# A convolution and a gated feed-forward layer on one core: reordering the kernel's first 20 microseconds

## The chip, the cores and the metric

One core of a Trainium2 chip runs the kernel. The metric is device time in microseconds (us), the median of several executions. Times inside the kernel are counted from the first instruction of one profiled execution. The engines are named PE or TensorE (matrix multiply; PEld are its weight loads), DVE or VectorE, ACT or ScalarE, POOL or GpSimd, and SP or SyncE, which here issues DMAs.

## The reference

```python
# x: (8, 4096, 192) float32, weight: (8, 7); moe_w_in: (192, 2048), moe_w_out: (2048, 192), moe_beta: (2048,)
w = softmax(weight, axis=-1)                          # 7 taps for each of 8 heads (24 channels a head)
x_pad = concatenate([zeros((8, 6, 192)), x], axis=1)  # causal: six rows of zeros ahead
conv[b, s, h, g] = sum_k w[h, k] * x_pad[b, s + k, h, g]
h = conv.reshape(32768, 192) @ moe_w_in
g = h * sigmoid(moe_beta * h)
out = g @ moe_w_out
```

## The kernel before, in words

The 32768 rows are cut into two streams (`s` = 0 and 1) of 16384 rows, worked side by side: stream 0 lives on partitions 0 to 63, stream 1 on 64 to 127. The 192 channels are split into three groups of 64 (`kk`), and the 2048 hidden columns into 16 chunks of 128 (`fc`).

Rows go in *steps*. Steps 0 and 1 have 128 rows of each stream, step 2 has 256, some more have 256 and 384, and the rest 512. For each step `i` and each unit `u` the first product (`mm1_pair` in steps 0 to 2, L326; `mm1` after them, L344) writes a PSUM buffer `ph`, of which there are two, and ScalarE applies Silu with the scale beta from `ph` to `g` (L330, L349). The second product (`mm2`, L377; later `mm2_quarters`, L423) sums over the 16 chunks in banks `po`; since the activation computes Silu(beta h) and not h sigmoid(beta h), `w_out` is divided by beta beforehand (`scale_w_out`, L274, one instruction for a chunk).

From step 3 on VectorE computes the convolution (`conv_ops`, L302 and L304) while TensorE multiplies. For the first 512 rows this would be too late, so TensorE does it: blocks 0 to 3 of 128 rows are transposed by TensorE (`transpose_0`, L216), copied to `xr` (`take_0`, L222 on ScalarE or L224 on VectorE), multiplied by seven diagonal matrices, one for each tap (`conv_0`, L230: a pair of matmuls for a tap, one for each stream), and brought to `xcp` with the softmax's denominator (`evac_0`, L239, L241). Block 0 feeds step 0, block 1 step 1, blocks 2 and 3 step 2. The diagonals (L200) come from the taps: a matmul spreads `taps` over the partitions (L191), VectorE takes the maximum (L193), ScalarE the exponential (L196).

Every instruction is pinned to its program order on its engine (`pin`). `first_tile(i, u)` is an order written out by hand: it says which pieces of convolution, evacuation and scaling stand behind unit `u` of steps 0 and 1. `first_mm2` does the same for the second product of steps 0 and 1: the table's entries name a pair of output blocks, the units (step, u) behind which its matmuls stand, and the cuts of the 16 chunks between them.

At the start `warm(n, cols)` issues `n` matmuls of a constant (L184) whose result nobody reads: fillers. Two stand ahead of the tap matmul (nine of 256 columns and one of 128), three between it and the transposes of block 0, and eight behind those.

The loads at the start: SP issues the taps, block 0 of stream 0, beta, and block 1; ACT issues block 0 of stream 1. GpSimd issues, in this order, `w_in` for its own half of the partitions (columns 0:256 and 256:640 of each half), blocks 2 and 3 of x, `w_in` 640:1024, four pieces of `w_out` (L157), the rows of the next tile (L159, L81), and then four copies of `w_in` from one half of the partitions to the other (L116). Steps 0 to 2 take each column from the half into which it was loaded; from step 3 on both halves are read.

Of the kernel before, what the change touches and what calls it, by code (L numbers as in the profile page):

```python
# [19 lines left out]
def kernel(  # L20
# [9 lines left out]
    nc = tc.nc  # L30

    B, S, D = x.shape
    H, K = weight.shape
# [3 lines left out]
    NF = F // 128  # L37
    NK = 3
    Q = D // NK
    NS = 2  # L40
# [3 lines left out]
    NB = TILE // 128  # L44

    def pin(ins):

        return tc.keep_in_program_order(ins)
# [35 lines left out]
    def cast_x(j, s, b0=0, b1=NB, eng=None):  # L84
        if j not in xbf_of:
            xbf_of[j] = xbf_pool.tile([128, NB, NK, NS, Q], BF16, name="xb")
        pin((eng or nc.vector).tensor_copy(  # L87
            xbf_of[j][:, b0:b1, :, s, :].rearrange("p b k q -> p k b q"),
            xf_of[j][:, b0:b1, s, :].rearrange("p b (q k) -> p k b q", k=NK)))

    def new_xt(j):
        xt_of[j] = xt_pool.tile([128, NK, LEAD + TILE], BF16, name="xt")

    def transpose_x(j, b):
        if j not in xt_of:
            new_xt(j)
        c = LEAD + 128 * b
        pin(nc.sync.dma_start_transpose(
            out=xt_of[j][:, :, c:c + 128],
            in_=xbf_of[j][:, b, :, :, :].rearrange("p k s q -> p (k s q)")))  # L100
# [4 lines left out]
    w_out_f = consts.tile([128, NF, D], FP32, name="w_out_f")  # L105
    w_out_s = consts.tile([128, NF, D], BF16, name="w_out_s")
    w_out_v = moe_w_out.rearrange("(c p) d -> p c d", p=128)

    def half_of(s):
        return slice(64 * s, 64 * s + 64)  # L110

    def load_w_in(s, f0, f1):
        pin(nc.gpsimd.dma_start(out=w_in_s[half_of(s), :, f0:f1], in_=w_in_v[:, :, f0:f1]))

    def copy_w_in(s, f0, f1):
        pin(nc.gpsimd.dma_start(out=w_in_s[half_of(1 - s), :, f0:f1], in_=w_in_s[half_of(s), :, f0:f1]))  # L116
# [3 lines left out]
    xb0 = consts.tile([128, 2, NS, D], BF16, name="xb0")  # L120
    xb1 = consts.tile([128, 2, NS, D], BF16, name="xb1")
    taps = consts.tile([H, K], FP32, name="taps")
    pin(nc.sync.dma_start(out=taps, in_=weight))
    for s, eng in enumerate((nc.sync, nc.scalar)):
        pin(eng.dma_start(out=x0[:, 0, s, :], in_=xs[s, 0:128, :]))
    beta16 = consts.tile([NF, 128], FP32, name="beta16")
    pin(nc.sync.dma_start(out=beta16, in_=moe_beta.rearrange("(c p) -> c p", p=128)))
    HF = F // 2

    def load_x0(b, eng):  # L130
        pin(eng.dma_start(out=x0[:, b, :, :] if b < 2 else xb0[:, b - 2, :, :],
                          in_=xs[:, 128 * b:128 * b + 128, :].rearrange("s p d -> p s d")))
# [14 lines left out]
                                pattern=[[0, NS], [-1, H], [0, Q // H]], channel_multiplier=1))  # L147
    pin(nc.gpsimd.affine_select(out=ident, in_=ident, compare_op=ALU.not_equal, fill=1.0,
                                base=0, pattern=[[-1, 128]], channel_multiplier=1))
    for f0, f1 in ((0, 256), (256, 640), (640, HF)):  # L150
        for s in range(NS):
            load_w_in(s, HF * s + f0, HF * s + f1)
        if f0 == 256:
            for b in range(2, NB):
                load_x0(b, nc.gpsimd)
    for c in range(0, NF, 4):
        pin(nc.gpsimd.dma_start(out=w_out_f[:, c:c + 4, :], in_=w_out_v[:, c:c + 4, :]))  # L157
    for s in range(NS):
        pin(nc.gpsimd.dma_start(out=xb1[:, :, s, :],  # L159
                                in_=xs[s, TILE:TILE + 256, :].rearrange("(b p) d -> p b d", p=128)))  # L160
# [12 lines left out]
    def po_banks():  # L173
        return [po_bank(), po_bank()]
# [7 lines left out]
    def warm(n, cols):  # L182
        for _ in range(n):
            pin(nc.tensor.matmul(idle[:, 0, 0:cols], ones[:, 0:128], ones[:, 0:cols], start=True, stop=True))  # L184

    warm(9, 256)
    warm(1, 128)
    cv0 = psum_h.tile([128, 2, TILE], FP32, name="ph")
    nmax = consts.tile([128, 1], FP32, name="nmax")
    tap_ps = cv0[:, 1, 0:K]  # L190
    pin(nc.tensor.matmul(tap_ps, sel.rearrange("h s g j -> h (s g j)"), taps, start=True, stop=True))  # L191
    warm(3, 128)
    pin(nc.vector.tensor_reduce(out=nmax, in_=tap_ps, axis=AX.X, op=ALU.max, negate=True))  # L193
    etap = consts.tile([128, K], FP32, name="etap")
    tsum = consts.tile([128, 1], FP32, name="tsum")
# [14 lines left out]
    def transpose_0(bank, src, b):  # L210

        bf = src.dtype == BF16
        t = (bank.bitcast(BF16) if bf else bank)[:, 0:NK * 128].rearrange("p (k t) -> p k t", k=NK)
        v = src[:, b, :, :].rearrange("p s d -> p (s d)").rearrange("p (m k) -> p k m", k=NK)
        for kk in range(NK):
            pin(nc.tensor.transpose(t[:, kk, :], v[:, kk, :], ident_b if bf else ident))  # L216
        return t

    def take_0(t, b, act=False):
        dst = xr[:, :, PAD + 128 * b:PAD + 128 * b + 128]  # L220
        if act:
            pin(nc.scalar.activation(dst, t, AF.Copy))  # L222
        else:
            pin(nc.vector.tensor_copy(dst, t))  # L224

    def conv_0(cv, b, k0=0, k1=K):

        for k in range(k0, k1):
            for s in range(NS):
                pin(nc.tensor.matmul(  # L230
                    cv[s][:, 0:NK * 128], diag[half_of(s), k, :, :].rearrange("p s q -> p (s q)"),
                    xr[half_of(s), :, 128 * b + k:128 * b + k + 128], start=(k == 0), stop=(k == K - 1)))

    def evac_0(cv, b, s, eng, k0=0, k1=NK):
        i, c = place[b]
        src = cv[s][:, 128 * k0:128 * k1].rearrange("p (k t) -> p k t", t=128)
        dst = xc_of[i][:, s, k0:k1, c:c + 128]
        if eng is nc.scalar:
            pin(nc.scalar.activation(dst, src, AF.Copy, scale=rsum))  # L239
        else:  # L240
            pin(eng.tensor_scalar_mul(dst, src, rsum))  # L241

    new_xt(0)
    pa = po_banks()
    pb = po_banks()
    t = transpose_0(pa[0], x0, 0)
    take_0(t, 0, act=True)
    warm(8, 128)
    for k in range(2, K):
        make_diag(k)  # L250
    rsum = consts.tile([128, 1], FP32, name="rsum")
    pin(nc.vector.reciprocal(rsum, tsum))
    for f in range(0, HF, 512):
        for s in range(NS):
            copy_w_in(s, HF * s + f, HF * s + f + 512)
    pin(nc.scalar.activation(scrap, one, AF.Silu))
    b0 = [cv0[:, 0, :], pb[0]]
    conv_0(b0, 0)
# [9 lines left out]
    rbeta = consts.tile([128, NF], FP32, name="rbeta")  # L268
# [1 line left out]
    tapn = consts.tile([128, K], FP32, name="tapn")  # L270
    pin(nc.vector.tensor_scalar_mul(tapn, etap, rsum))

    def scale_w_out(c):
        pin(nc.vector.tensor_scalar_mul(w_out_s[:, c, :], w_out_f[:, c, :], rbeta[:, c:c + 1]))  # L274


    def conv_ops(i):
# [224 lines left out]
    def first_tile(i, u):  # L502
        if (i, u) == (0, 1):
            conv_0(pb, 1, 0, 4)
        elif (i, u) == (0, 2):
            conv_0(pb, 1, 4, K)
        elif (i, u) == (0, 3):
            t23 = [transpose_0(pa[b], xb0, b) for b in range(2)]
            for b in range(2):
                take_0(t23[b], 2 + b)  # L510
            for s in range(NS):
                evac_0(pb, 1, s, nc.vector)
        elif (i, u) == (0, 5):
            conv_0(pa, 2, 0, 4)
            for c in range(4):
                scale_w_out(c)
        elif (i, u) == (0, 6):
            conv_0(pa, 2, 4, K)
            for s in range(NS):
                evac_0(pa, 2, s, nc.vector)  # L520
            for c in range(4, 8):
                scale_w_out(c)
        elif (i, u) == (1, 0):
            conv_0(pb, 3, 0, 4)
        elif (i, u) == (1, 1):
            conv_0(pb, 3, 4, K)
            for s in range(NS):
                evac_0(pb, 3, s, nc.vector)
            for c in range(8, NF):
                scale_w_out(c)  # L530
        elif (i, u) == (1, 6):
            new_xt(1)
            ts_ = [transpose_0(pb[b], xb1, b) for b in range(2)]
            for b in range(2):
                pin(nc.vector.tensor_copy(xt_of[1][:, :, LEAD + 128 * b:LEAD + 128 * b + 128], ts_[b]))
            pin(nc.vector.tensor_copy(xt_of[0][:, :, TILE + LEAD - PAD:],
                                      xr[:, :, TILE:].bitcast(FP32)))
        elif (i, u) == (1, 7):
            for s in range(NS):
                cast_x(1, s, 2, NB)  # L540
            for b in range(2, NB):
                transpose_x(1, b)
            for j in (2, 3):
                for s in range(NS):
                    load_x(j, s)
# [2 lines left out]

    prs_0 = ((0, 0), (1, 0))
    first_mm2 = {}  # L550
    for key, us, cuts in (((0, 0), [(1, u) for u in range(2, 8)], (0, 3, 6, 9, 12, 13, 16)),
                          ((1, 0), [(2, 1), (2, 2)], (0, 8, 16)),
                          ((0, 1), [(2, 3), (2, 4)], (0, 8, 16)),
                          ((1, 1), [(2, 5), (2, 6), (2, 7)], (0, 5, 10, 16))):
        for (i, u), c0, c1 in zip(us, cuts, cuts[1:]):
            first_mm2[(i, u) + key] = range(c0, c1)

    for i in range(n_steps):
# [16 lines left out]
        for u in range(0, NF, du):  # L575
            us = range(u, u + du)
# [41 lines left out]
```

## Time and profile before

| | |
|---|---|
| median of 5 runs | 686.37 us (685.61 to 687.11) |
| profiled execution | 686.4 us, of which 684.5 us are the span from first to last instruction |
| busy share of the span | PE 99%, PEld 67%, DVE 80%, ACT 85%, POOL 2% |
| granted TensorE clock | 1.00 |
| first activation of step 0 (L330) | starts at 8.79 us |
| last activation of step 1 | ends at 22.03 us |
| first product of step 3 (L344) | starts at 30.66 us |
| GpSimd's DMA issues | from 1.72 to 12.90 us, its copies of `w_in` at 13.23, 14.44, 15.64 and 18.38 us |

The profile shows one execution. A busy TensorE is not TensorE at its peak, since matmuls are pipelined and their ends are modelled. A line of a timeline gives the start, the busy time, the engine, the line of the kernel, the operation and its tiles, how many were merged, and in brackets the idle time of the engine before it with what ended it. A line can be that of a helper. The names of tiles in the trace leave out buffer numbers, so that `x0`, `xb0` and `xb1` read `x` and `xb`.

### The profile page before, as it was taken

The numbers are of one execution on the slowest core, as the hardware profiler recorded it, in microseconds if no ns is written. First come the engines' busy times: TensorE is split into PE (matmuls) and PEld (weight loads), VectorE is DVE, ScalarE is ACT, GpSimd is POOL, SyncE is SP. The second block draws the span as 40 slices with busy tenths as digits, with TensorE's granted clock in tenths as the row PEclk, the third lists the DMA queues.
The fourth block names the chain that finished last, engine by engine and source line by source line (L and its number), as shares of the span: only waits on it lengthen the run. The fifth ranks groups of instructions, "written<-read, shape, count | busy, mean of one in ns | idle before, by whom it ended". The sixth has DMA issues, their size and how long they took to land.

```text
span 684.5 us, 27214 instructions
## 1 busy us (share of the span) xinstructions
PE 680.1 (99%) x12530; PEld 461.5 (67%) x12530; DVE 550.9 (80%) x886; ACT 583.9 (85%) x585; POOL 14.5 (2%) x26
## 2 busy tenths in 40 slices
PE   9999999999999999999999999999999999999998
PEld 7799887666666666666666666666666666666667
DVE  5999999999988889878889888889888889875112
ACT  7999999888888888888888888888888888888881
POOL 8000000000000000000000000000000000000000
PEclk9999999999999999999999999999999999999999
DMA  9643434444432334423344323344324443220223
GB/s 202 186 129 91 125 103 115 94 117 118 115 78 67 106 106 117 117 56 82 106 112 117 100 64 91 100 118 117 93 51 106 104 118 71 53 64 5 49 48 94
DMA packets 150418, 66.85 MB, mean 98 GB/s; under 512 B 113648, under 2 KB 149696, under 8 KB 150304
## 3 DMA queue, kind: packets, MB, share of 16 engines
q1 hardware_dynamic: 146992, 61.08, 35.1%
q0 software_dynamic: 3168, 3.93, 2.8%
q8 instruction: 98, 1.61, 1.0%
q14 instruction: 16, 0.13, 0.1%
q10 hardware_dynamic: 144, 0.10, 0.0%
HBM read 28.32 MB, written 25.17 MB: 78 GB/s over the span
## 4 chain that ended last, share of the span: by engine, by line
PE 99%; ACT 0%; DVE 0%; issue 0%
PE ph L344 47%; PE po L423 43%; PE po L377 4%; PE ph L326 2%; PE po L461 2%; PE po L230 1%; PE ph L184 1%; ACT gp L330 0%; PE ph L230 0%; PE po L216 0%; PE ph L191 0%; DVE o_sp L383 0%; PE po L264 0%
## 5 line engine op out<-in xcount | busy, mean ns | idle before, releaser
L349 ACT ACTIVATE g<-ph,beta 128x1024 bf16<-128x1024 f32 (+2 forms) x528 | 557.3, 1063 | 80.8 <-PE ph L344 61.8
L344 PE MATMUL ph<-xc,w_in_s 64*64 64x512 bf16 (+3 forms) x5952 | 612.3, 368 | 0.0
L423 PE MATMUL po<-g,w_out_s 64*64 64x512 bf16 (+1 forms) x5568 | 580.0, 372 | 0.0
L344 PEld LDWEIGHTS <-w_in_s 64*64 64x64 bf16 (+1 forms) x5952 | 275.2, 104 | 125.5 <-issue 0.4
L423 PEld LDWEIGHTS <-w_out_s 64*64 64x64 bf16 x5568 | 290.2, 118 | 84.0
L304 DVE SCALAR_TENSOR_TENSOR acc<-xt,tapn,acc 128x512 f32<-128x512 bf16 (+2 forms) x450 | 311.2, 764 | 0.9
L440 DVE STREAM_TRANSPOSE o_sb<-po 128x512 f32<-128x512 f32 (+1 forms) x87 | 76.3, 877 | 111.7 <-PE po L423 111.7
L304 DVE SCALAR_TENSOR_TENSOR xc<-xt,tapn,acc 128x512 bf16<-128x512 bf16 (+2 forms) x90 | 64.1, 765 | 0.2
L87 DVE CAST xb<-xf 128x768 bf16<-128x768 f32 (+1 forms) x62 | 48.5, 822 | 0.0
L302 DVE TENSOR_SCALAR acc<-xt,tapn 128x512 f32<-128x512 bf16 (+2 forms) x90 | 41.0, 486 | 1.1
L377 PE MATMUL po<-w_out_s,g 64*128 64x192 bf16 x512 | 28.3, 243 | 0.0
L377 PEld LDWEIGHTS <-g 64*128 64x128 bf16 x512 | 23.5, 94 | 1.6
L383 DVE COPY o_sp<-po 128x192 f32<-128x192 f32 x28 | 9.0, 353 | 8.5 <-PE po L461 7.3
L326 PE MATMUL ph<-xcp,w_in_s 64*128 64x256 bf16 (+1 forms) x144 | 14.9, 306 | 0.2
L330 ACT ACTIVATE gp<-ph,beta 128x256 bf16<-128x256 f32 x32 | 12.6, 478 | 1.2 <-PE ph L326 0.9
L461 PEld LDWEIGHTS <-g 128*128 128x128 bf16 x128 | 10.5, 98 | 0.4 <-issue 0.4
L461 PE MATMUL po<-w_out_s,g 128*128 128x192 bf16 x128 | 10.7, 246 | 0.0
L330 ACT ACTIVATE g<-ph,beta 128x512 bf16<-128x512 f32 x16 | 9.6, 693 | 0.1
L326 PEld LDWEIGHTS <-w_in_s 64*128 64x128 bf16 x144 | 6.8, 94 | 3.5 <-issue 1.6
L230 PE MATMUL po<-xr,diag 64*128 64x384 f32 x49 | 7.8, 379 | 0.0
L377 PE MATMUL po<-w_out_s,gp 64*128 64x192 bf16 x128 | 7.6, 243 | 0.0
L377 PEld LDWEIGHTS <-gp 64*128 64x128 bf16 x128 | 5.9, 94 | 1.6
(52 smaller groups left out, 59.4 us busy)
## 6 DMA issues: line engine op xcount, KB each, us to landing
xf<-in_x_dram SPq DMA_DIRECT2D x60, 384.0 KB, 4.1
out_dram<-o_sb SPq DMA_DIRECT2D x108, 192.0 KB, 4.7
xt<-xb SPq DMA_TRANSPOSE x122, 3.1
out_dram<-o_sp SPq DMA_DIRECT2D x10, 192.0 KB, 3.8
w_out_f<-in_moe_w_out_dram POOLq DMA_DIRECT2D x4, 384.0 KB, 6.6
out_dram<-o_sb SPq DMA_DIRECT2D x8, 144.0 KB, 4.0
w_in_s<-w_in_s POOLq DMA_DIRECT2D x4, 192.0 KB, 7.1
out_dram<-o_sp SPq DMA_DIRECT2D x8, 96.0 KB, 1.8
```

Source lines behind the costliest of these rows:

```text
L87: pin((eng or nc.vector).tensor_copy(xbf_of[j][:, b0:b1, :, s, :].rearrange("p b k q -> p k b q"), xf_of[j][:, b0:b1, s, :].rearrange("p b ...
L230: pin(nc.tensor.matmul(cv[s][:, 0:NK * 128], diag[half_of(s), k, :, :].rearrange("p s q -> p (s q)"), xr[half_of(s), :, 128 * b + k:128 * ...
L302: pin(nc.vector.tensor_scalar_mul(a, src, w))
L304: pin(nc.vector.scalar_tensor_tensor(out=xc_of[i][:, k0:k1, o:o + m] if k == K - 1 else a, in0=src, scalar=w, in1=a, op0=ALU.mult, op1=ALU ...
L326: pin(nc.tensor.matmul(ph[:, h, 0:NS * n], w_in_s[half_of(h), kk, ts(fcs[h], 128)], xc_of[i][half_of(h), :, kk, :], start=(kk == 0), stop= ...
L330: pin(nc.scalar.activation(g_at(i, fcs[h])[:, :, 0:n], ph[:, h, 0:NS * n].rearrange("p (s t) -> p s t", s=NS), AF.Silu, scale=beta[:, fcs[ ...
L344: pin(nc.tensor.matmul(ph[m0:m1, s, n * e:n * e + n], w_in_s[half_of(s), kk, 128 * fc + m0:128 * fc + m1], xc_of[i][half_of(s), kk, 0:n], ...
L349: pin(nc.scalar.activation(g_at(i, fc)[:, :, 0:n], ph[:, :, n * e:n * e + n], AF.Silu, scale=beta[:, fc:fc + 1]))
L377: pin(nc.tensor.matmul(po[q][:, 0:D], g_at(i, fc)[r, s, ts(b, 128)], w_out_s[r, fc, :], start=(phase == 0 and fc == 0), stop=(phase == 1 a ...
L423: pin(nc.tensor.matmul(po_of[i, m][half_of(s), 0:n], w_out_s[half_of(r), fc, m:D:NM], g_at(i, fc)[half_of(r), s, 0:n], start=(first and fc ...
L440: pin(nc.vector.transpose(osb_of[i][:, 0:n // L, :, m], po_of[i, m][:, 0:n].rearrange("p (b l) -> p b l", l=L)))
L461: pin(nc.tensor.matmul(po[:, 0:D], g_at(i, fc)[:, s, ts(b, 128)], w_out_s[:, fc, :], start=(fc == 0), stop=(fc == NF - 1)))
```

## The change

The taps are loaded behind block 0 of x, on ACT's queue instead of SP's. GpSimd loads `w_in` in pieces of 256, 192, 192 and 384 columns for each half, all of them ahead of blocks 2 and 3 of x. The fillers become six of 256 columns ahead of the tap matmul, none between it and the transposes, and six of 128 columns behind these. The transposes of blocks 2 and 3 and the copies from them stand behind two units, (0,3) and (0,4), instead of one; their tap runs stand behind (0,5) and (0,7), and (1,1) and (1,3). GpSimd does the scaling of chunks 8 to 15 of `w_out`, ahead of its copies of `w_in`; VectorE does that of 0 to 7. The second product of the first pair of step 0 stands behind (1,4), (1,5), (1,7) and (2,0).

```diff
--- before.py
+++ after.py
@@ -120,9 +120,9 @@
     xb0 = consts.tile([128, 2, NS, D], BF16, name="xb0")
     xb1 = consts.tile([128, 2, NS, D], BF16, name="xb1")
     taps = consts.tile([H, K], FP32, name="taps")
-    pin(nc.sync.dma_start(out=taps, in_=weight))
     for s, eng in enumerate((nc.sync, nc.scalar)):
         pin(eng.dma_start(out=x0[:, 0, s, :], in_=xs[s, 0:128, :]))
+    pin(nc.scalar.dma_start(out=taps, in_=weight))
     beta16 = consts.tile([NF, 128], FP32, name="beta16")
     pin(nc.sync.dma_start(out=beta16, in_=moe_beta.rearrange("(c p) -> c p", p=128)))
     HF = F // 2
@@ -147,12 +147,11 @@
                                 pattern=[[0, NS], [-1, H], [0, Q // H]], channel_multiplier=1))
     pin(nc.gpsimd.affine_select(out=ident, in_=ident, compare_op=ALU.not_equal, fill=1.0,
                                 base=0, pattern=[[-1, 128]], channel_multiplier=1))
-    for f0, f1 in ((0, 256), (256, 640), (640, HF)):
+    for f0, f1 in ((0, 256), (256, 448), (448, 640), (640, HF)):
         for s in range(NS):
             load_w_in(s, HF * s + f0, HF * s + f1)
-        if f0 == 256:
-            for b in range(2, NB):
-                load_x0(b, nc.gpsimd)
+    for b in range(2, NB):
+        load_x0(b, nc.gpsimd)
     for c in range(0, NF, 4):
         pin(nc.gpsimd.dma_start(out=w_out_f[:, c:c + 4, :], in_=w_out_v[:, c:c + 4, :]))
     for s in range(NS):
@@ -183,13 +182,11 @@
         for _ in range(n):
             pin(nc.tensor.matmul(idle[:, 0, 0:cols], ones[:, 0:128], ones[:, 0:cols], start=True, stop=True))
 
-    warm(9, 256)
-    warm(1, 128)
+    warm(6, 256)
     cv0 = psum_h.tile([128, 2, TILE], FP32, name="ph")
     nmax = consts.tile([128, 1], FP32, name="nmax")
     tap_ps = cv0[:, 1, 0:K]
     pin(nc.tensor.matmul(tap_ps, sel.rearrange("h s g j -> h (s g j)"), taps, start=True, stop=True))
-    warm(3, 128)
     pin(nc.vector.tensor_reduce(out=nmax, in_=tap_ps, axis=AX.X, op=ALU.max, negate=True))
     etap = consts.tile([128, K], FP32, name="etap")
     tsum = consts.tile([128, 1], FP32, name="tsum")
@@ -245,14 +242,11 @@
     pb = po_banks()
     t = transpose_0(pa[0], x0, 0)
     take_0(t, 0, act=True)
-    warm(8, 128)
+    warm(6, 128)
     for k in range(2, K):
         make_diag(k)
     rsum = consts.tile([128, 1], FP32, name="rsum")
     pin(nc.vector.reciprocal(rsum, tsum))
-    for f in range(0, HF, 512):
-        for s in range(NS):
-            copy_w_in(s, HF * s + f, HF * s + f + 512)
     pin(nc.scalar.activation(scrap, one, AF.Silu))
     b0 = [cv0[:, 0, :], pb[0]]
     conv_0(b0, 0)
@@ -270,8 +264,14 @@
     tapn = consts.tile([128, K], FP32, name="tapn")
     pin(nc.vector.tensor_scalar_mul(tapn, etap, rsum))
 
-    def scale_w_out(c):
-        pin(nc.vector.tensor_scalar_mul(w_out_s[:, c, :], w_out_f[:, c, :], rbeta[:, c:c + 1]))
+    def scale_w_out(c, eng=nc.vector):
+        pin(eng.tensor_scalar_mul(w_out_s[:, c, :], w_out_f[:, c, :], rbeta[:, c:c + 1]))
+
+    for c in range(NF // 2, NF):
+        scale_w_out(c, nc.gpsimd)
+    for f in range(0, HF, 512):
+        for s in range(NS):
+            copy_w_in(s, HF * s + f, HF * s + f + 512)
 
 
     def conv_ops(i):
@@ -504,30 +504,27 @@
             conv_0(pb, 1, 0, 4)
         elif (i, u) == (0, 2):
             conv_0(pb, 1, 4, K)
-        elif (i, u) == (0, 3):
-            t23 = [transpose_0(pa[b], xb0, b) for b in range(2)]
-            for b in range(2):
-                take_0(t23[b], 2 + b)
-            for s in range(NS):
-                evac_0(pb, 1, s, nc.vector)
-        elif (i, u) == (0, 5):
-            conv_0(pa, 2, 0, 4)
-            for c in range(4):
-                scale_w_out(c)
-        elif (i, u) == (0, 6):
-            conv_0(pa, 2, 4, K)
-            for s in range(NS):
-                evac_0(pa, 2, s, nc.vector)
-            for c in range(4, 8):
-                scale_w_out(c)
-        elif (i, u) == (1, 0):
-            conv_0(pb, 3, 0, 4)
-        elif (i, u) == (1, 1):
-            conv_0(pb, 3, 4, K)
-            for s in range(NS):
-                evac_0(pb, 3, s, nc.vector)
-            for c in range(8, NF):
-                scale_w_out(c)
+        elif (i, u) in ((0, 3), (0, 4)):
+            if u == 3:
+                for s in range(NS):
+                    evac_0(pb, 1, s, nc.vector)
+            take_0(transpose_0((pa, pb)[u - 3][0], xb0, u - 3), u - 1)
+        elif (i, u) in ((0, 5), (0, 7)):
+            k0, k1 = ((0, 4), (4, K))[u == 7]
+            conv_0(pa, 2, k0, k1)
+            if u == 7:
+                for s in range(NS):
+                    evac_0(pa, 2, s, nc.vector)
+                for c in range(5):
+                    scale_w_out(c)
+        elif (i, u) in ((1, 1), (1, 3)):
+            k0, k1 = ((0, 4), (4, K))[u == 3]
+            conv_0(pb, 3, k0, k1)
+            if u == 3:
+                for s in range(NS):
+                    evac_0(pb, 3, s, nc.vector)
+                for c in range(5, NF // 2):
+                    scale_w_out(c)
         elif (i, u) == (1, 6):
             new_xt(1)
             ts_ = [transpose_0(pb[b], xb1, b) for b in range(2)]
@@ -548,7 +545,7 @@
 
     prs_0 = ((0, 0), (1, 0))
     first_mm2 = {}
-    for key, us, cuts in (((0, 0), [(1, u) for u in range(2, 8)], (0, 3, 6, 9, 12, 13, 16)),
+    for key, us, cuts in (((0, 0), [(1, 4), (1, 5), (1, 7), (2, 0)], (0, 3, 5, 10, 16)),
                           ((1, 0), [(2, 1), (2, 2)], (0, 8, 16)),
                           ((0, 1), [(2, 3), (2, 4)], (0, 8, 16)),
                           ((1, 1), [(2, 5), (2, 6), (2, 7)], (0, 5, 10, 16))):
```

## The prediction, made before the changed kernel was run

> **What bounds the kernel now.** I read the chain that ended last first, because it says whether this change can reach the end at all.
>
> ```profile
> PE 99%; ACT 0%; DVE 0%; issue 0%
> ...
> 22.08 0.82 PE ph L326 x6
> 22.91 0.66 PE po L377 x16
> ...
> 30.82 0.67 PE ph L344 x12
> 31.49 0.66 PE po L377 x16
> ```
>
> The lower lines are the same chain in order of time: start, length, what. From 22.08 us on TensorE goes from one group straight to the next until the end, and nothing of the change touches the loop after 30.8. So the change is worth what it does to the moment at which TensorE stands at 22.08, plus work it moves behind that moment. Which wait ends last before 22.08 is in ScalarE's timeline (start, busy, engine, line, operation; in brackets the idle time before it and its releaser).
>
> ```profile
> 4.59 0.49 ACT L222 ACTIVATE xr<-po 128x384 fp32r<-128x384 f32 x1 [0.51 <-PE po L216]
> 7.52 0.73 ACT L239 ACTIVATE xcp<-ph,rsum 128x128 bf16<-128x128 f32 x2 [0.92 <-PE po L230]
> 8.79 4.83 ACT L330 ACTIVATE gp<-ph,beta 128x256 bf16<-128x256 f32 x12 [0.54 <-PE ph L326]
> 13.96 8.07 ACT L330 ACTIVATE gp<-ph,beta 128x256 bf16<-128x256 f32 x20 [0.34 <-PE ph L326]
> ```
>
> The 32 activations of steps 0 and 1 take 0.403 us each (4.83/12 and 8.07/20), 12.90 in all; with one gap of 0.34 they run from 8.79 to 22.03, and TensorE's next PSUM buffer comes free then. So 22.03 = 8.79 + 12.90 + 0.34: only an earlier first activation and that gap can be won. The first activation hangs on TensorE's opening.
>
> ```profile
> 0.78 2.19 PE L184 MATMUL ph<-const-bfloat16-1.0 128*128 128x256 bf16 x10 [0.78 <-PEq L602]
> 2.89 0.59 PE L191 MATMUL ph<-taps,sel 8*128 8x7 f32 x2
> 3.42 0.50 PE L184 MATMUL ph<-const-bfloat16-1.0 128*128 128x128 bf16 x3
> 3.71 0.85 PE L216 MATMUL po<-ident,x 128*128 128x128 f32 x3
> 4.35 1.06 PE L184 MATMUL ph<-const-bfloat16-1.0 128*128 128x128 bf16 x8
> ...
> 6.46 0.49 PE L230 MATMUL ph<-xr,diag 64*128 64x384 f32 x1
> ...
> 6.79 0.34 PE L230 MATMUL ph<-xr,diag 64*128 64x384 f32 x1
> ...
> 6.97 0.34 PE L230 MATMUL ph<-xr,diag 64*128 64x384 f32 x1
> ```
>
> The reader is to see two things. Fillers (L184) leave TensorE no hole from 0.78 on. And the tap pairs (L230) start 0.32 us apart up to 6.79 and 0.18 apart after it, with the same shape: TensorE's pace rises at 6.79, after 6.01 us of almost unbroken work, although the row of granted clock reads full speed from the start.
>
> **Part by part.** The sum is made against the profiled execution: 686.4 us, of which 684.5 are the span and 1.9 lie around it; the median of the runs is 686.37, so both stand for the same.
>
> *Taps behind x.* The taps' DMA goes from first on SP (0.74) to second on ACT; SP's second issue was at 1.21, so I take that. The x halves took 1.9 and 2.0 us to land, and the first one now on SP lands near 2.7 instead of 3.2. The taps' landing isn't printed. If it takes 1.9 they are there at 3.1; if the tap matmul at 2.89 (its weight load comes after 0.30 of idle) started on their arrival, they took 2.15 and are there at 3.36. The transposes stay behind the tap matmul in TensorE's order, so x first alone moves nothing. They follow it by 0.53 instead of 0.71, since three fillers go. Net: 3.1 + 0.53 - 3.60 = +0.03, or 3.36 + 0.53 - 3.60 = +0.29. I take +0.25, near the second, because the idle before 2.89 fits a wait. With taps at once it would be -0.2. The issue of 0.39 on ACT also moves the Exp table load (1.16 for 1.28) to about 1.6-2.9; the first Exp is due after 3.9, so this is hidden. Beta and block 1 come 0.4 earlier on SP; nobody waits for them.
>
> *Fillers.* Three of 256 columns, one and three of 128 and two of 128 go. They started 0.214 us apart at 256 columns, so about 0.107 at 128: 3 x 0.214 + 6 x 0.107 = 1.28 us of work, and TensorE now stands from 2.06 (0.78 + 6 x 0.214) to about 3.3, and again 0.2 before the tap pairs. The fillers themselves were covered by waits, so their time is no gain. What they bought may be the step at 6.79. The trace doesn't show a hole, so bounds: no shift, 0; or the count of 6.01 us starts again at 3.36, the step comes at 9.37, and 2.58 us of work run at 0.18/0.32 of the pace, which costs 2.58 x 0.44 = 1.13. The work in that stretch (the last pairs, the transposes of block 1, L326, the next tap pairs) is the TensorE part of the chain up to 11.16, so it is not covered. Between the two, if only the 1.28 us of missing work count, 1.28 x 0.44 = 0.56. A rise that comes earlier gives at most the four slow pairs (5.34 to 6.79, 1.45 against 4 x 0.18 = 0.72), -0.73, and 0.10 on block 0's transposes (0.64 in the chain, block 1's 0.54). I take +1.13, because the only row there is has the rise after unbroken work.
>
> [...]
>
> *Pool's queue.* L113 issues went 0.62-0.75 apart. Two more pieces, all eight ahead of x blocks 2 and 3, put block 2's issue from 4.32 to about 1.72 + 0.75 + 7 x 0.62 = 6.8. It landed in 4.8, the last w_in piece in 5.4, so block 2 is there at 11.6 (11.3 if the transfers and not the issues set it: the same bytes were all in at 6.42 + 5.4 = 11.8). Its transposes ran at 11.05, so TensorE would wait up to 0.55 there, at (0,3). That takes the place of the old gap of 0.34, which came from tap pairs waiting at 12.56 for the second VectorE take that began the same round (L224, 11.51 for 1.02); spreading transposes and tap runs one to a unit removes it. Bounds -0.34 and +0.6 (0.55 less 0.34, and tap pairs of 0.82 plus L326 of 0.34 in a unit of 0.81 with no lead left); I take 0, since with the later start above TensorE asks for block 2 after it has landed and the tap run at (0,5) takes the slack. Smaller pieces cost no transfer time that I can see: 444 packets, 389 of them under 512 B, moved in the slice 8-9 us, against 201 larger ones in 9-10.
>
> *Behind it in the queue.* w_out, block pairs and xf are issued 2 x 0.62 = 1.25 later. They landed 5.9 to 8.8 us after issue, against 4.1 for the first: they queue on transfers, so the issue is hidden. If it weren't, xf would land at 22.1 for a VectorE cast that began at 21.12, the taps of step 3 (finished at 30.14) end 1.0 later, 0.5 past TensorE's need at 30.66: 0 to +0.5, taken 0.
>
> *GpSimd's eight scales.* VectorE did eight in 1.93 us and then idled 0.54 for TensorE, so their absence there gains nothing. GpSimd's nearest row is a 128x128 select in 0.28, hence 0.42 for 192 columns; VectorE's row is 0.31, and I bound at 0.24 and 1.0. The fourth w_out piece landed at 9.33 + 8.8 = 18.1 (19.4 if issue-bound); four scales of 0.42 end at 19.8 (21.1). The last consumer now is (2,0), near 21.8, so it is covered; at 1.0 each and the later landing it ends at 23.4, a stall of 1.6. Taken 0. The four w_in copies wait behind the scales: issued near 20 to 23 instead of 13.2 to 18.4, landing 4.5 to 8.1 later, the first by 28.7; step 3 needs it at 30.66. Cover 2 us.
>
> [...]
>
> *Output matmuls moved.* Twelve of the first pair's go from step 1, where ScalarE sets the pace, to (2,0), ahead of 22.08. At 0.66/16 = 0.041 each they are 0.49; TensorE idled 0.32 before 22.08, so +0.17 (0 to +0.49).
>
> **Sum.** 0.25 + 1.13 + 0 + 0 + 0.17 = +1.55: 686.4 + 1.55 = 687.95, said as 688.0.
>
> **The rivals.** *The pace rises where it did.* Then 0.25 + 0.17 = +0.4: 686.8, no change that counts. For it: 1 us of hole in 6 us need not matter. Against it: the fillers' exact fit in the old trace.
>
> *Faster.* The pace rises early: all tap pairs run at 0.18 (-0.73) and block 0's transposes too (-0.10); taps land with x (-0.2), the 0.34 goes and the moved matmuls fit the hole (0): -1.37, 685.0. It decides if the rise falls before about 3.9. For it: the runs before differ by 1.5 us, so something in the opening is not fixed. Against it: less work stands ahead of the rise.
>
> *Data late.* Block 2 lands 1.5 later than I put it, or the scales end at 23.4: +1.5 on the +0.4 and more, 688.3 to 689.5. Against it: packets got cheaper, not dearer, when they were smaller.
>
> **How the numbers follow.** A measurement of this kernel can tell about 0.2%, 1.4 us, from no change: 685.0 and 687.7 are the bounds. Forecast 0.40 (slower); data late 0.12 (slower); pace unchanged or hardly later 0.35 (same); faster 0.13. So faster 0.13, same 0.35, slower 0.52. The range reaches from 685.6 (the faster case cut, some 0.1 left out) to 689.2 (the dearest of the late cases left out). The forecast's own range is 687.2 (taps 0.03, pace 0.56, matmuls 0.17) to 688.3 (0.29, 1.13, 0.49); its part under 687.7 is counted in the 0.35.
>
> **What would show it.** Right: tap pairs still 0.32 apart after 6.79 and the pace rising near 9.4; transposes starting near 3.85; first L330 activation near 9.6 to 9.9; hole-free activations to about 22.9; TensorE reaching L344 about 1.5 us later than 30.82. Wrong, if the spacing falls to 0.18 before 7 us (then the first rival), if activations begin before 8.5 (faster), or if a gap of over 1 us stands at (0,3), (1,7) or (2,0) with a DMA or GpSimd as its releaser (data late).

## The result and the profile after

The changed kernel took 687.86 us (25 runs, 687.25 to 690.54) against 686.45 for the kernel before on the same chips: 1.0024 times its time, 95% interval 1.0019 to 1.0030, or +1.4 us. The forecast was 688.0, slower. The number came out; the experiments show that two of the terms behind it did not, and that it was luck in part: timed a second time (a_repeat) the changed kernel took 687.46, under the 687.7 from which the forecast counted as slower.

The profiled execution was one of the slowest, 690.21 us with a span of 688.4. First its chain that ended last, by engine:

```profile
PE 92%; DVE 4%; DMA 2%; issue 1%; ACT 1%; SPq 0%; ACTq 0%; DVEq 0%
```

VectorE and a DMA stand in a chain that was TensorE's at 99% before. TensorE's opening (start, busy, engine, line, operation, idle before and its releaser):

```profile
0.76 1.44 PE L183 MATMUL ph<-const-bfloat16-1.0 128*128 128x256 bf16 x6 [0.76 <-PEq L599]
3.48 0.56 PE L189 MATMUL ph<-taps,sel 8*128 8x7 f32 x2 [1.27 <-DMA taps<-in_weight_dram]
3.97 0.91 PE L213 MATMUL po<-ident,x 128*128 128x128 f32 x3
...
7.23 0.52 PE L227 MATMUL ph<-xr,diag 64*128 64x384 f32 x1
...
7.55 0.52 PE L227 MATMUL ph<-xr,diag 64*128 64x384 f32 x1
```

The taps are now what TensorE waits for, and the tap pairs are still 0.32 apart at 7.55. ScalarE's run through steps 0 and 1, and the start of step 2:

```profile
9.37 4.67 ACT L330 ACTIVATE gp<-ph,beta 128x256 bf16<-128x256 f32 x12 [0.54 <-PE ph L326]
14.42 3.02 ACT L330 ACTIVATE gp<-ph,beta 128x256 bf16<-128x256 f32 x8 [0.38 <-PE ph L326]
17.63 4.62 ACT L330 ACTIVATE gp<-ph,beta 128x256 bf16<-128x256 f32 x12 [0.19 <-PE ph L326]
22.47 1.26 ACT L330 ACTIVATE g<-ph,beta 128x512 bf16<-128x512 f32 x2 [0.22 <-PE ph L326]
```

The first activation is 0.58 later than before, but the run ends at 22.25, only 0.22 later. What was added after that is in the timelines of GpSimd, TensorE and VectorE:

```profile
16.67 6.41 POOL L268 TENSOR_SCALAR w_out_s<-w_out_f,rbeta 128x192 bf16<-128x192 f32 x8 [2.55 <-DVE w_out_s L268]
23.03 2.53 POOL L116 DMA_DIRECT2D w_in_s<-w_in_s  x4
```

```profile
23.13 0.26 PE L377 MATMUL po<-w_out_s,gp 64*128 64x192 bf16 x2 [0.29 <-POOL w_out_s L268]
23.21 0.82 PE L326 MATMUL ph<-xcp,w_in_s 64*128 64x512 bf16 x6
```

```profile
33.98 0.85 DVE L87 CAST xb<-xf 128x768 bf16<-128x768 f32 x1 [2.72 <-DMA xf<-in_x_dram]
35.19 0.84 DVE L87 CAST xb<-xf 128x768 bf16<-128x768 f32 x1 [0.35 <-DMA xf<-in_x_dram]
```

The same casts in the kernel before:

```profile
30.06 1.61 DVE L87 CAST xb<-xf 128x768 bf16<-128x768 f32 x2
```

Eight scales take 6.41 us, 0.80 each. TensorE waits 0.29 for the last one, and the copies of `w_in` leave only at 23.03. VectorE's cast for the next tile, at 30.06 before, stands until 33.98 for rows that are issued at 25.35, while these copies are on their way (they land between 26.28 and 33.10), and VectorE, whose instructions are pinned to their order, has the convolution of step 4 behind it (from 36.47, before from 32.09). Matched matmul by matmul, TensorE is 1.12 late at 33 us and 3.64 late at 65.

### The profile page after: what moved, and what is told of

Its sections match the earlier page's. It is cut to its first block, busy times and chain, and to the rows that moved or that the text cites. A ratio compares the mean times of both kernels' runs of the same rounds, so it can differ in the third digit from the quotient of the medians.

```text
span 688.4 us, 27199 instructions
## 1 busy us (share of the span) xinstructions
PE 680.6 (99%) x12521; PEld 463.8 (67%) x12521; DVE 550.3 (80%) x878; ACT 583.8 (85%) x585; POOL 22.1 (3%) x36
## 4 chain that ended last, share of the span: by engine, by line
PE 92%; DVE 4%; DMA 2%; issue 1%; ACT 1%; SPq 0%; ACTq 0%; DVEq 0%
PE ph L344 45%; PE po L423 43%; DVE acc L304 2%; PE po L461 2%; DMA xf<-in_x_dram 1%; PE po L377 1%; PE ph L326 1%; ACT gp L330 1%; DVE o_sp L383 1%; DVE acc L302 1%; PE po L227 0%; PE ph L227 0%; DVE xb L87 0%; PE po L213 0%; DMA taps<-in_weight_dram 0%
## 5 line engine op out<-in xcount | busy, mean ns | idle before, releaser
L344 PE MATMUL ph<-xc,w_in_s 64*64 64x512 bf16 (+3 forms) x5952 | 594.4, 368 | 0.6 <-DVE xc L304 0.6
L423 PE MATMUL po<-g,w_out_s 64*64 64x512 bf16 (+1 forms) x5568 | 561.2, 372 | 0.0
L344 PEld LDWEIGHTS <-w_in_s 64*64 64x64 bf16 (+1 forms) x5952 | 272.6, 105 | 122.4 <-PE po L377 0.8
L423 PEld LDWEIGHTS <-w_out_s 64*64 64x64 bf16 x5568 | 285.0, 118 | 84.6
L330 ACT ACTIVATE gp<-ph,beta 128x256 bf16<-128x256 f32 x32 | 12.2, 482 | 1.2 <-PE ph L326 1.1
L330 ACT ACTIVATE g<-ph,beta 128x512 bf16<-128x512 f32 x16 | 9.9, 688 | 0.7 <-PE ph L326 0.6
L238 DVE TENSOR_SCALAR xcp<-po,rsum 128x384 bf16<-128x384 f32 (+2 forms) x8 | 4.2, 562 | 6.1 <-PE po L227 6.1
```

The costliest lines, as they stand in the source:

```text
L330: pin(nc.scalar.activation(g_at(i, fcs[h])[:, :, 0:n], ph[:, h, 0:NS * n].rearrange("p (s t) -> p s t", s=NS), AF.Silu, scale=beta[:, fcs[ ...
L344: pin(nc.tensor.matmul(ph[m0:m1, s, n * e:n * e + n], w_in_s[half_of(s), kk, 128 * fc + m0:128 * fc + m1], xc_of[i][half_of(s), kk, 0:n], ...
L423: pin(nc.tensor.matmul(po_of[i, m][half_of(s), 0:n], w_out_s[half_of(r), fc, m:D:NM], g_at(i, fc)[half_of(r), s, 0:n], start=(first and fc ...
```

## Experiments

Each was timed in five rounds beside the kernel before, which had 686.39, 686.50 and 686.40 us in the three sets. Rise is the moment at which the trace's record of a granted TensorE clock of 1.00 begins. In the profile before it begins at 6.79, where the spacing of the tap pairs drops from 0.32 to 0.18; in a_fill's, where it begins at 5.31, the pairs stand 0.18 apart from 5.71 on, and in the changed kernel's, with 8.11, 0.32 apart to the last at 7.55 (the page's row of granted clock, which reads 1.00 from the start, does not show it).

| kernel | median us | ratio, 95% interval | rise | first L330 | step 3 |
|---|---|---|---|---|---|
| before | 686.4 | | 6.79 | 8.79 | 30.66 |
| changed | 687.86 | 1.0024 (1.0019-1.0030) | 8.11 | 9.37 | 31.78 |
| a_repeat | 687.46 | 1.0017 (1.0008-1.0026) | 9.01 | 9.49 | 31.53 |
| a_dve | 687.53 | 1.0016 (1.0007-1.0025) | 7.12 | 8.97 | 31.15 |
| a_half | 687.24 | 1.0009 (1.0000-1.0018) | 9.68 | 9.80 | 31.67 |
| a_fill | 687.67 | 1.0021 (1.0013-1.0030) | 5.31 | 8.25 | 31.50 |
| a_dve_mm2 | 687.70 | 1.0016 (1.0008-1.0025) | 7.96 | 9.41 | 31.77 |
| a_dve_ord | 687.42 | 1.0013 (1.0004-1.0021) | 7.63 | 9.28 | 31.25 |
| a_dve_open | 687.15 | 1.0010 (1.0001-1.0019) | 9.69 | 9.79 | 31.69 |
| b_fill | 686.55 | 1.0002 (0.9993-1.0011) | 6.89 | 8.46 | 30.48 |
| b_pool | 687.97 | 1.0024 (1.0015-1.0034) | 5.20 | 8.11 | 31.28 |
| b_taps | 687.87 | 1.0021 (1.0012-1.0030) | 10.02 | 10.24 | 32.04 |
| b_spread | 686.23 | 0.9997 (0.9988-1.0006) | 6.81 | 8.81 | 30.74 |
| best | 687.00 | 1.0006 (0.9997-1.0015) | 9.73 | 9.57 | 31.55 |

The last three columns are of one execution each. Names in a_ start from the changed kernel, those in b_ and best from the kernel before. The diffs are shortened: comments and words in brackets stand for lines that are left out.

### First set: pace or scales?

The pace theory is the forecast's (fewer fillers, later rise). The scale theory came from the profile above.

**a_dve**

```diff
-    for c in range(NF // 2, NF):
-        scale_w_out(c, nc.gpsimd)
+    # VectorE: c 0-3 behind (0,6), 4-7 (0,7), 8-11 (1,1), 12-15 (1,3)
```

> The changed kernel, but VectorE scales all 16 chunks again: four behind (0,6), four behind (0,7), four behind (1,1), four behind (1,3). The copies of w_in no longer queue behind scales. Scale theory (GpSimd's eight scales take 0.80 us each, end at 23.08, TensorE waits for the last of them and the w_in copies come out only then): TensorE is at the first unit of step 2 about 0.9 earlier, 686.6 to 686.9 us, and the spread above 689 goes. Pace theory (the later rise of TensorE's pace, the step of +1.13 in the forecast): nothing of it is touched, 687.6 to 688.0.

687.53: the runs above 688.5 are gone (the highest is 687.84), but most of the loss stays. Scale theory explains the tail and not the bulk. VectorE's row for its scales 4 to 11:

```profile
16.23 2.05 DVE L268 TENSOR_SCALAR w_out_s<-w_out_f,rbeta 128x192 bf16<-128x192 f32 x8
```

**a_fill**

```diff
-    warm(6, 256)
+    warm(12, 256)
```

> The changed kernel with 12 fillers of 256 columns ahead of the tap matmul instead of 6, so that TensorE has no hole while it waits for the taps (0.78 to about 3.35). Pace theory: the rise comes as early as before, 686.7 to 687.0. Scale theory: the first activation comes up to 0.5 earlier, but TensorE still waits for the scale that ends near 23.1, so 687.6 to 687.9.

687.67. In its profile the rise came at 5.31 and the first activation at 8.25, earlier than before the change, and still TensorE was late at step 3. Its and VectorE's waits:

```profile
11.16 0.35 PE L213 MATMUL po<-ident_b,xb 128*128 128x128 bf16 x3 [0.58 <-DMA xb<-in_x_dram]
...
22.85 0.26 PE L377 MATMUL po<-w_out_s,gp 64*128 64x192 bf16 x2 [0.55 <-POOL w_out_s L268]
```

```profile
32.62 0.86 DVE L87 CAST xb<-xf 128x768 bf16<-128x768 f32 x1 [1.64 <-DMA xf<-in_x_dram]
```

In this execution the early TensorE waits 0.58 for block 2 of x and then 0.55 for the scales, against 0 and 0.29 in the changed kernel's first profile. So most of what its early rise gave was gone by step 3: 0.54 ahead of the kernel before at the first activation, 0.84 behind it there.

**b_pool**

```diff
+    for c in range(NF // 2, NF):
+        scale_w_out(c, nc.gpsimd)          # ahead of the copies of w_in
-            for c in range(8, NF):
-                scale_w_out(c)
```

> The kernel before, with one part of the change alone: GpSimd scales chunks 8 to 15, ahead of the copies of w_in. Here the second product wants chunks 9 to 15 already behind (1,5) to (1,7), near 19 to 21 us. Scale theory: scales of 0.80 from about 15.3 end near 22 and stall TensorE in step 1, 687.2 to 689 us, with the copies near 22. Pace theory: 686.3 to 686.6, since no filler is touched.

687.97, inside what the scale theory expected, although the first activation of its profile was 0.68 earlier than before: scales from 15.54 to 21.7 and copies from 21.66.

```profile
15.54 6.17 POOL L271 TENSOR_SCALAR w_out_s<-w_out_f,rbeta 128x192 bf16<-128x192 f32 x8 [2.62 <-DMA w_out_f<-in_moe_w_out_dram]
21.66 2.59 POOL L116 DMA_DIRECT2D w_in_s<-w_in_s  x4
```

**b_fill**

```diff
-    warm(9, 256); warm(1, 128); (tap matmul); warm(3, 128); (transposes); warm(8, 128)
+    warm(6, 256); (tap matmul); (transposes); warm(6, 128)
```

> The kernel before, with the fillers of the change alone: six of 256 columns, none between the tap matmul and the transposes, six of 128. The taps stay first on SP, so the hole on TensorE is 2.06 to about 2.9. Pace theory: the rise comes 1.3 to 2.5 us later, 687.0 to 687.6. Scale theory: the opening is worth at most 0.3, 686.3 to 686.8.

686.55, not to be told from the kernel before, and under the 687.0 of the pace theory. TensorE's opening in its profile:

```profile
2.46 0.56 PE L190 MATMUL ph<-taps,sel 8*128 8x7 f32 x2 [0.24 <-DMA taps<-in_weight_dram]
3.19 0.88 PE L214 MATMUL po<-ident,x 128*128 128x128 f32 x3 [0.16 <-DMA x<-in_x_dram]
3.86 0.84 PE L184 MATMUL ph<-const-bfloat16-1.0 128*128 128x128 bf16 x6
4.65 0.68 PE L228 MATMUL ph<-xr,diag 64*128 64x384 f32 x1
```

With the taps first on SP they are there at 2.46, and the tap pairs start at 4.65, 0.69 earlier than before. In this execution the rise came 0.10 later than before and the first activation 0.33 earlier. So the run holds a gain beside whatever a later rise costs, and 686.55 is the sum of the two; it does not measure the pace alone. In the kernel before, the fillers and not the taps were what the tap matmul waited for at 2.89.

### Second set: what is left without the scales

**a_dve_mm2**

```diff
-((0, 0), [(1, 4), (1, 5), (1, 7), (2, 0)], (0, 3, 5, 10, 16))
+((0, 0), [(1, 4), (1, 5), (1, 6), (1, 7)], (0, 4, 8, 11, 16))     # on a_dve
```

> The changed kernel with all scales on VectorE, and the second product of the first pair kept wholly in step 1: chunks 0-3 behind (1,4), 4-7 behind (1,5), 8-10 behind (1,6), 11-15 behind (1,7), none behind (2,0). Sum theory (the 1.1 us that the kernel with VectorE scales is still behind are twelve matmuls moved behind step 1, about 0.5, the opening, about 0.2, and block 2's later landing, about 0.3): 687.0 to 687.2. Spread theory (the spreading of the tap runs alone makes ScalarE wait in units (0,6) to (1,1)): 687.4 to 687.6, since TensorE stands no better at step 2's first unit.

687.70: no gain. The matmuls' place behind (2,0) is not a cause of the loss. Between the middle of step 1 and step 2 (from 19 to 26 us) ScalarE loses about a third of a microsecond against the kernel before in both (a_dve from 0.15 to 0.49 late, a_dve_mm2 from 0.79 to 1.11). The way there differs: up to 21 us a_dve gains 0.09 and a_dve_mm2 loses 0.16, and behind it they lose 0.43 and 0.16. What the matmuls cost behind (2,0) they had freed in step 1.

**a_dve_ord**

```diff
-for f0, f1 in ((0, 256), (256, 448), (448, 640), (640, HF)):   ... blocks 2, 3 last
+for f0, f1 in ((0, 256), (256, 640), (640, HF)):               ... blocks 2, 3 after the second
```

> The changed kernel with all scales on VectorE, and GpSimd's loads as before the change: w_in in pieces of 256, 384, 384 columns, blocks 2 and 3 of x after the second. Sum theory: block 2 has landed before (0,3), the wait of 0.3 to 0.4 goes, 687.1 to 687.3. Spread theory: 687.4 to 687.6.

687.42, 0.1 under a_dve: inconclusive by time, but the profiles agree on the wait. In a_dve block 2's transposes stand for its landing, in a_dve_ord they do not:

```profile
11.67 0.35 PE L213 MATMUL po<-ident_b,xb 128*128 128x128 bf16 x3 [0.36 <-DMA xb<-in_x_dram]
```

**a_dve_open**

```diff
+    pin(nc.sync.dma_start(out=taps, in_=weight))      # first on SP, on a_dve
-    pin(nc.scalar.dma_start(out=taps, in_=weight))
+    warm(9, 256); warm(1, 128) ... warm(3, 128) ... warm(8, 128)
```

> The changed kernel with all scales on VectorE, and the opening as before the change: taps first on SP, fillers 9 of 256 and 1 of 128, then 3, then 8. Sum theory: tap matmul back at 2.9, the first activation 0.2 earlier, but then a longer wait for block 2, so 687.3 to 687.5. Pace theory: 686.4 to 686.7. Spread theory: 687.4 to 687.6.

687.15, the largest step back of the three (0.38 under a_dve), between what two theories expected; the intervals overlap.

**b_spread**

```diff
+ transposes of blocks 2, 3 behind (0,3), (0,4); tap runs behind (0,5), (0,7), (1,1), (1,3)
+ scales on VectorE as in a_dve; first pair's second product as in a_dve_mm2
```

> The kernel before with the spread alone: transposes of blocks 2 and 3 behind (0,3) and (0,4), tap runs behind (0,5), (0,7), (1,1), (1,3), scales on VectorE behind (0,6), (0,7), (1,1), (1,3), second product of the first pair behind (1,4) to (1,7). Opening, loads and fillers as before. Sum theory: the old gap of 0.34 in ScalarE's run goes and nothing takes its place, 686.0 to 686.3. Spread theory: 687.0 to 687.4.

686.23, the same as the kernel before. The spread costs nothing, but the gap of 0.34 did not go either: its profile has one of 0.38 at the same activation. Spread theory falls.

```profile
13.85 3.03 ACT L331 ACTIVATE gp<-ph,beta 128x256 bf16<-128x256 f32 x8 [0.38 <-PE ph L327]
```

Matched activation by activation, ScalarE is 0.01 behind the kernel before at the first one, 0.27 ahead at 15 us and 0.08 behind at 22: the spread does shorten the waits of step 0, and the gain is gone by step 2.

### Third set: the taps, half the scales, a second look

**b_taps**

```diff
-    pin(nc.sync.dma_start(out=taps, in_=weight))      # ahead of block 0
+    pin(nc.scalar.dma_start(out=taps, in_=weight))    # behind it, on ACT
```

> The kernel before with the taps' load alone moved: behind block 0 of x on ACT's queue, fillers as before. Taps theory: the tap matmul at 3.4 instead of 2.9, block 0's transposes 0.5 later because the three fillers between still stand, and the stall of 0.27 near 577 us that the profiles with the taps on ACT show: 686.9 to 687.3. If the taps' place is worth only what the forecast gave it (0.25): 686.5 to 686.8.

687.87: this part alone costs as much as the whole change, above even the higher expectation's range. TensorE's opening and the first activations:

```profile
3.42 0.56 PE L191 MATMUL ph<-taps,sel 8*128 8x7 f32 x2 [0.45 <-DMA taps<-in_weight_dram]
3.91 0.50 PE L184 MATMUL ph<-const-bfloat16-1.0 128*128 128x128 bf16 x3
4.20 0.85 PE L216 MATMUL po<-ident,x 128*128 128x128 f32 x3
...
5.83 0.69 PE L230 MATMUL ph<-xr,diag 64*128 64x384 f32 x1
```

```profile
10.24 4.77 ACT L330 ACTIVATE gp<-ph,beta 128x256 bf16<-128x256 f32 x12 [1.03 <-PE ph L326]
```

The tap matmul is 0.53 later than before, the transposes and the first tap pair 0.49, and in this execution the rise came at 10.02. The first activation is 1.45 later: 0.49 of it at most are the taps' own, the rest goes with the rise.

**a_half**

```diff
-    for c in range(NF // 2, NF):
+    for c in range(12, NF):                # 8-11 on VectorE behind (1,1)
         scale_w_out(c, nc.gpsimd)
```

> The changed kernel with only chunks 12 to 15 scaled by GpSimd, 8 to 11 by VectorE behind (1,1), 0 to 7 by VectorE behind (0,6) and (0,7). Scale theory: four scales of 0.75 after the last w_out piece has landed near 17.6 end near 20.9, before TensorE asks near 22.2; the copies come out 2 us earlier than in the changed kernel: the level of the kernel with all scales on VectorE, 687.3 to 687.6, and hardly an execution above 688.5. If it is any arithmetic on GpSimd that costs, and not its end: 687.8 to 688.0 with the same spread.

687.24, no run above 687.71, and GpSimd is done before TensorE asks:

```profile
16.85 3.17 POOL L268 TENSOR_SCALAR w_out_s<-w_out_f,rbeta 128x192 bf16<-128x192 f32 x4 [2.74 <-DVE xcp L238]
19.98 2.53 POOL L116 DMA_DIRECT2D w_in_s<-w_in_s  x4
```

So the cost is not in any arithmetic on GpSimd, but in when it ends and when the copies behind it leave.

**a_repeat**, the changed kernel unchanged.

> The changed kernel itself again, for a second profile, since the first was of one of its slowest executions (690.2 against a median of 687.9). Scale theory: GpSimd's scales again take 0.75 to 0.80 each and end near 23, TensorE reaches step 3 about 1.1 later than in the kernel before; if the xf loads behind the copies of w_in land before VectorE wants them, the execution is near 687.8, and if not, near 690. Pace theory: the slow executions are those with a late rise of TensorE's pace.

687.46; the profiled execution took just that. GpSimd, TensorE and VectorE again:

```profile
16.34 6.07 POOL L268 TENSOR_SCALAR w_out_s<-w_out_f,rbeta 128x192 bf16<-128x192 f32 x8 [2.22 <-DMA w_out_f<-in_moe_w_out_dram]
22.36 2.53 POOL L116 DMA_DIRECT2D w_in_s<-w_in_s  x4
```

```profile
22.48 0.66 PE L377 MATMUL po<-w_out_s,gp 64*128 64x192 bf16 x12
22.98 0.81 PE L326 MATMUL ph<-xcp,w_in_s 64*128 64x512 bf16 x6
```

```profile
32.27 0.86 DVE L87 CAST xb<-xf 128x768 bf16<-128x768 f32 x1 [0.49 <-DMA xf<-in_x_dram]
```

Here the scales ended at 22.4, TensorE, later itself with the rise at 9.01, did not wait, and VectorE waited only 0.49. A late rise is thus not what made 690.2: that one had its rise at 8.11, this one at 9.01.

**best**

```diff
-    warm(3, 128)                           # on b_spread
```

> The spread alone on the kernel before, and no fillers between the tap matmul and block 0's transposes; taps first on SP, loads as before, scales on VectorE. The spread measured 0.27 under the kernel before and the removal of fillers brought the first activation 0.33 earlier in its profile: 685.9 to 686.2 if they add, 686.2 to 686.5 if TensorE's own work fills the time.

687.00: neither expectation. It is no better than the kernel before; its profiled execution had its rise at 9.73. No version measured here beats the kernel before.

## Why the prediction was right, and where its steps were not

**The whole.** In the typical execution (a_repeat's profile, 687.46) matched against the one before: the first activation +0.70, step 3 at +0.87, the end +1.15; the last 0.27 comes behind 669 us (see the last section), where the forecast had nothing. The 690.2 execution adds 2.5 between 33 and 65 us. Of the signs that the forecast gave, the spacing of 0.32 behind 6.79 and the start of the transposes came; the first activation was earlier than its 9.6 to 9.9, and the activations were not free of gaps. The forecast's sign and size hold, for a cause it shares only in part. The size is luck in part: the opening was put too high, and two costs that stood at 0, that of the end of the run and that of the late copies, made up for it.

**Taps, +0.25: size right in place, reason wrong.** Block 0's transposes start at 3.84 (a_repeat) and 3.97 (changed) against 3.71: +0.13 and +0.26. At the tap pairs, with two fillers fewer behind the transposes, -0.01 and +0.12 are left of it. And I took the idle before 2.89 for a wait for the taps, and b_fill shows them there by 2.46. The move to second on ACT made them arrive about 1 us later, near 3.4; the kernel before had that slack filled with fillers. Alone it costs 1.0021 times (1.0012 to 1.0030), the dearest single part of the opening; but in b_taps' profile more than half of that goes with the late rise, so taps and pace are not two separate terms.

**Pace, +1.13: the right wait, too large, and the fillers not shown to be its cause.** In a_repeat the tap pairs start where they did before, so the whole +0.70 of the first activation goes with the rise, 2.22 later; in the changed kernel's first profile 0.58 less at most 0.12 go with a rise 1.32 later. The price is near: with the old opening the rise at 6.79 and at 9.69 (before, a_dve_open) gave first activations at 8.79 and 9.79, 1.00/2.90 = 0.34 per microsecond against my 0.44. The late one, in a_dve_open, where the last tap pairs start at 7.11 and 7.43, still 0.32 apart:

```profile
9.79 4.62 ACT L330 ACTIVATE gp<-ph,beta 128x256 bf16<-128x256 f32 x12 [1.07 <-PE ph L326]
```

The shift is not what I said. In the changed kernel the rise came at 8.11 and 9.01, 1.3 and 2.2 later than before, not 2.58; and with the old opening it came at 5.20, 6.79, 6.81 and 9.69. So it moves from execution to execution by more than the term: one and the same opening shows rises 4.5 us apart.

A typical size is only an estimate, from the runs' own scatter. If the runs of one kernel differ by the rise alone, at 0.34 per microsecond, the median run of a_dve, a_dve_ord, a_dve_mm2 and a_half, which have the changed opening and no long wait for scales, had its rise between 8.0 and 8.5, and that of the kernel before at about 6.9: 0.4 to 0.5 us, less than half of the 1.13. The kernel before itself falls into two groups, 110 of its 143 runs up to 686.84 and 33 from 687.00 to 687.32; late rises would explain the second, but no profile was taken of it.

The fillers alone (b_fill) gave +0.16 with an interval from -0.5 to +0.75. With what its earlier tap pairs gain at an equal rise, about 0.36 (0.33 and 0.10 of rise), a later rise can cost from -0.1 to +1.1 there: the test does not settle it. What the profiles have in common is TensorE's wait ahead of the tap matmul. In the seven in which it stood 0.45 to 1.33 for the taps, the rise came 3.7 to 6.6 behind the tap matmul. That it waits for 6.01 us of work, counted again from there, was my assumption from the one profile before; a spread of 2.9 is no fixed count, and no run shows what sets the rise. Of the seven others five had it between 5.20 and 6.89, but two, with no such wait, at 9.69 and 9.73. That the wait makes late rises more frequent fits, and stays open: one profile a kernel is too few to tell.

**GpSimd's scales, 0: mis-sized.** The 0.42 from the select's 0.28 was measured as 0.75 to 1.00, mean 0.80; they end at 23.08 and not 19.8. The bound of 1.0 held it, the value did not. An early TensorE waits (0.55 in a_fill, 0.29 in the changed kernel's profile), a late one (a_repeat) does not, so the wait eats what an early rise would give; between the medians of the changed kernel and a_dve lie 0.33. VectorE's own scales were slower beside them: in the changed kernel's profile five of the seven that ran while GpSimd scaled took 0.40 to 0.47 each, against a median of 0.31 before. VectorE's scales come about 0.25 apart (2.05 for eight in a_dve), most of GpSimd's 0.75.

**The copies of w_in: the wrong deadline.** I asked when step 3 needs them, and that held. I didn't ask what they would meet: the loads of the next tile's rows, issued from 25.35. Their landing took 8.6 us in the changed kernel's profile, against 3.8 to 4.3 for the first ones before; the xt transfer issued ahead of them on SP's queue, at 23.97, was as slow, 8.4 against 2.4. VectorE then waits 2.72 in front of step 4's convolution. Of 58 runs of the four kernels with eight scales ahead of the copies (changed, a_repeat, a_fill, b_pool) 11 were above 688.5; of 99 runs of the other nine experiments none. That is the rival "data late", with another transfer than the one I named.

**Block 2, 0: right.** In the changed kernel's two profiles no matmul waits for it; where TensorE came earlier it waited 0.36 (a_dve) and 0.58 (a_fill), about the 0.55 given. But the 0.34 did not go away: a gap of 0.38 stands at the same place, and what the spread gains in step 0 is lost again by step 2 (b_spread). Why was not tested; the tap run behind (0,5) is as long as before. And 0.403 was not ScalarE's own pace, as I read it: undisturbed activations start 0.365 apart, and the small TensorE waits between them were inside that mean.

**Matmuls moved, +0.17: not seen.** Undoing it gained nothing (687.70 against 687.53). I had them cost behind (2,0) and gain nothing in step 1; a_dve and a_dve_mm2 show about 0.25 on each side. The 0.32 of idle that I set against them was that of the weight loads.

**The parts do not add.** Taps +1.5, fillers +0.2, scales +1.6 and spread -0.3, each alone on the kernel before, make 2.9 before rounding; together they cost 1.4. Two overlaps show in the profiles: without fillers between tap matmul and transposes the late taps delay the tap pairs less (0.12 and not 0.49), and a late TensorE no longer waits for the scales (a_repeat). That they make up the whole difference was not tested.

## What to carry to other kernels

When a load is pushed down a queue, measure when it lands against when it is asked for with the padding taken out: fillers ahead of a wait can make a transfer look critical that is early (here the taps, asked for at 2.89 before, and there by 2.46 in b_fill), or hide one that is about to be (a_fill's tap matmul at 3.41, with no wait). A transfer that is delayed within its deadline still needs a second question: which other transfers will now be under way at the same time, and which engine, pinned to its order, waits for those (here VectorE, for 2.72). Where parts of a change overlap in time, time each alone and do not expect the sum. And where an execution's own luck, here the moment of the rise (5.20 to 9.69 with one opening, 1.0 at the first activation between 6.79 and 9.69), is worth as much as the change, one profile is one draw: compare many runs.

## What the runs showed that was not expected

In all eight profiles with the taps on ACT's queue one activation near 577 us starts 0.28 late, and in none of the six others. Here in a_repeat and, unstretched, before:

```profile
577.91 2.12 ACT L349 ACTIVATE g<-ph,beta 128x1024 bf16<-128x1024 f32 x2 [0.52 <-PE ph L344]
```

```profile
576.75 2.35 ACT L349 ACTIVATE g<-ph,beta 128x1024 bf16<-128x1024 f32 x2 [0.24 <-PE ph L344]
```

ScalarE's idle time there is 0.52 instead of 0.24. That alone costs nothing: matched with the kernel before, a_repeat's activations are 0.88 late ahead of it, 1.15 at it and 0.88 again two activations later, and so they stay up to the last one. What stays changed is how TensorE's matmuls of the first product (L344) and the second (L423) alternate. Just ahead of it their starts go in twos and fours by turns in both kernels; at the end of the run they still do in the kernel before, but in a_repeat they go in groups of twelve. The time is lost when the first product is over, where a longer run of the second is left, again a_repeat and before:

```profile
669.10 2.54 PE L423 MATMUL po<-g,w_out_s 64*64 64x512 bf16 x28
```

```profile
668.38 2.11 PE L423 MATMUL po<-g,w_out_s 64*64 64x512 bf16 x24
```

All eight have the 28 and end 0.25 to 0.29 later than their last activations would give; the others have the 24, and 0.02 or less. One more instruction at the start of ACT's program goes with it; why it shows 570 us later was not found.
